# A fused attention and MLP kernel: the order of work at its two changeovers

## The chip, the cores and the metric

One core of a Trainium2 chip. The metric is the device time of one execution in microseconds (us); lower is better. Engines are named as in the profile: PE (TensorE matmul; PEld its weight loads), DVE (VectorE), ACT (ScalarE), POOL (GpSimd) and SP (SyncE, here the queue that issues nearly all DMAs).

## The reference

Random-feature attention, then an MLP with a residual, all float32 in and out (weights arrive as float64 and are decoded in the kernel).

```python
# attention: q, k, v are (8, 8, 576, 64), omega (128, 64)
h = (x * D**-0.25) @ omega.T - sum(x * x) / 2        # for q and for k
phi = exp(h - max(h)) / sqrt(m)
out = phi_q @ (phi_k.T @ v) / (phi_q @ sum(phi_k) + 1e-6)
# mixing and MLP: x is (8, 576, 512), U (576, 32), V (32, 576), w1 (512, 2048), w2 (2048, 512)
u = x + (x.transpose(0, 2, 1) @ U @ V).transpose(0, 2, 1)
return u + maximum(u @ w1, 0) @ w2
```

## The kernel before

**Stages.** Attention runs first, in rounds over pairs of batches and heads. A generator `mixing` (L302) does the U and V products of a pair and stores `u` to memory (`u_dram`, nine chunks of 512 rows). Then comes layer 1 (`u @ w1`, relu), whose result `g` goes to memory (`g_dram`), and layer 2 (`g @ w2` plus `u`).

**Products.** Each float32 product is made of three matmuls of rounded halves: an operand is split into a high part (a cast on ACT, `wh`, `uh`, `gh`) and a low part (value minus high, `wl`, `ul`, `gl`). Both layers use a two-by-two block scheme with 7 products instead of 8 and extra sums: of the left operand S1 to S4 (`SUMS`, L171), of the right operand T1 to T4 (`Right.sums`, L724), and of results. The order of the operands is in `LEFT` and `RIGHT`.

**Layer 1.** Work is cut into units (`unit`, L787) of one chunk c and one weight group g (four groups, NG = 4; nine chunks, NCH = 9). A unit has 7 products of 12 matmuls, 84 in all (L821). DVE adds them (L811), ACT copies and relus (L826, L807), SP stores (L801). Each unit yields after each product, and the caller puts other work there. The order is chunk by chunk, groups 0 to 3. The right operands of a chunk (`prepare`, L749) are 16 loads, 4 transposes on DVE (L768), 4 sums on POOL (L729) and 7 splits (L736, L737); they lie in 8 buffers each of `uh` and `ul`, 7 of them for a chunk.

**Weights.** `decoding` (L101) turns float64 pieces of 128 x 512 into float32: a load (L166) into `raw`, of which there are two buffers (`RB`), two ACT operations (`magnitude`, L114 and L117), three DVE slots (L133, L134, L137) and an addition on POOL (L155). Each call of `advance` does one slot. Four pieces make a group of w1; its operands are 4 sums (L204), 7 casts (L210) and 7 lows (L214) for each of two halves. For groups 0 and 1 sums and lows are on POOL, during attention; for groups 2 and 3 they are on DVE. Group 2's first half is kept in `held` until room for it is free. The 16 pieces of w2 are decoded during layer 1 and go through memory (`w2_dram`).

**First changeover.** `opening` (L848) lays units (0, 0) and (0, 1) between the last mixing steps, with 11 slots of decoding. Unit (0, 2) follows when group 2 is made, (0, 3) when group 3 is.

**Second changeover.** In the last chunk's four units the operands of w2 (`prepare_w2`, L890, and `Right.split`, L733) replace those of w1, one product after another; all four sums are on POOL and the lows alternate between DVE and POOL. When layer 1 is over, the operands of layer 2's first step are made.

**Layer 2.** 36 steps of 7 products and 84 matmuls each (L1043). `Step.split` (L964) makes the operands for the next step while this one runs: a cast on ACT (L976), a low on DVE (L977), S3 and S1 on POOL and S2 and S4 on DVE (L962). S2 is made ahead of split 4 and used in split 5, S4 ahead of split 5 and used in split 6. `Post` (L980) adds the results of two steps to `u` and stores them, between the products of the step after.

**What sets the order.** `K` (`tc.keep_in_program_order`) pins an instruction behind all that was traced before it on its engine. What is not pinned, all DMAs and parts of the decoding among it, may be moved ahead by the framework's scheduler. Each engine then runs its queue strictly in order. PSUM banks come in two sets that alternate from unit to unit (`banks`, L783).

Of the kernel before, what the change touches and what calls it, by code (L numbers as in the profile page):

```python
# [29 lines left out]
def performer_mlp_kernel(ctx: ExitStack, tc, q, k, v, omega, U, V, w1, w2, out):  # L30
# [70 lines left out]
    def decoding(jobs, late, lean):  # L101


        raws, mags, lows = {}, {}, {}

        def fetch(i):
            if i < len(jobs):
                raws[i] = dec.tile([P, PIECE, 2], U32, name="raw", bufs=RB)[:, : jobs[i][1], :]
                jobs[i][0](raws[i])
# [9 lines left out]
        for i in range(RB):  # L119
            fetch(i)  # L120
# [4 lines left out]
        for i, job in enumerate(jobs):  # L125
# [19 lines left out]
            for j, slot in enumerate(slots):  # L145
# [5 lines left out]
                if j == len(slots) - 1:  # L151
                    fetch(i + RB)
# [11 lines left out]
    def weights(src, dest, after):  # L164
        def load(raw):
# [9 lines left out]
    wops, made, held = {}, set(), []  # L175
# [5 lines left out]

    def w1_jobs(g):
        for half in range(2):
            tiles = {}

            def dest(c, tiles=tiles):
                if not tiles:
                    tiles["w"] = dec.tile([P, 2, PIECE], F32, name="wf", bufs=2)
                return tiles["w"][:, c, :]

            def value(name, tiles=tiles):
                w = tiles["w"]
# [6 lines left out]
            engine = nc.gpsimd if g < EARLY_GROUPS else nc.vector

            def total(_, name, value=value, tiles=tiles, engine=engine):
                x, y, op = SUMS[name]
                tiles[name] = dec.tile([P, 2 * P], F32, name="ws", bufs=4)
                engine.tensor_tensor(out=tiles[name], in0=value(x), in1=value(y), op=op)  # L204

            after = [lambda w, name=name, total=total: total(w, name) for name in SUMS]
            for i, name in enumerate(LEFT):

# [9 lines left out]
            if g == EARLY_GROUPS and half == 0:  # L218
                held.extend(after)
                after = []  # L220
# [868 lines left out]
```

## Time and profile before

| | us |
|---|---|
| median of 3 runs | 1136.36 |
| lowest, highest | 1133.68, 1137.52 |
| profiled execution, own time | 1135.71 |
| its span, first to last instruction | 1133.8 |
| mean granted TensorE clock | 0.973 of full |
| busy: PE, DVE, ACT, POOL | 1057.1, 888.8, 612.7, 498.3 |

The span is what the views of the profile cover; the execution's own time has 1.9 us more. A busy share is an average over stages with different limits, so stages are read by their own stretches. "X <- Y" in a list of waits means that X's engine sat idle until Y was done.

### The profile page before, as it was taken

How to read it: one execution, taken by the hardware profiler on the slowest of the kernel's cores; microseconds unless marked ns; L12 is line 12 of the kernel's file. 1: busy time of each engine (PE TensorE's matmuls, PEld its weight loads, DVE VectorE, ACT ScalarE, POOL GpSimd, SP SyncE). 2: the span in 40 equal slices, each digit the busy share in tenths (PEclk: the TensorE clock that was granted, in tenths of full speed). 3: DMA queues.
4: the chain of work that ended last, by engine and by line, in shares of the span. 5: the costliest groups of instructions: out<-in, count | busy, mean ns of one | idle time of the engine just before them, and what ended most of it. 6: DMA issues, size and time to landing. Idle time of an engine off the chain costs nothing. (4 is left out here: it accounts for less than half of the span.)

```text
span 1133.8 us, 23916 instructions
## 1 busy us (share of the span) xinstructions
PE 1057.1 (93%) x8497; PEld 1028.6 (91%) x8497; DVE 888.8 (78%) x1553; ACT 612.7 (54%) x1464; POOL 498.3 (44%) x433
## 2 busy tenths in 40 slices
PE   8989989999988579999999999979999999999998
PEld 7989878899978479899889999869999999999998
DVE  4888899897998885755645555669999999999995
ACT  4878878889863554543433443555443444444441
POOL 3436768737333233123121012575655454554542
PEclk9899999999998789999999999998999999999999
DMA  7788586485245568677666445435453544444351
GB/s 129 142 153 148 95 191 143 89 190 107 81 94 158 161 174 222 168 205 188 188 183 150 119 123 131 143 107 198 144 188 125 172 153 166 170 143 162 143 183 41
DMA packets 374902, 169.25 MB, mean 149 GB/s; under 512 B 275168, under 2 KB 348896, under 8 KB 370176
## 3 DMA queue, kind: packets, MB, share of 16 engines
q1 hardware_dynamic: 374720, 167.67, 55.9%
q8 instruction: 67, 1.10, 0.4%
q14 instruction: 51, 0.42, 0.1%
q0 software_dynamic: 64, 0.07, 0.0%
HBM read 106.86 MB, written 60.82 MB: 148 GB/s over the span
## 5 line engine op out<-in xcount | busy, mean ns | idle before, releaser
L567 ACT ACTIVATE e<-p_p,nm 128x128 f32<-128x128 f32 x576 | 166.5, 386 | 25.0 <-DVE nm L560 15.7
L976 ACT CAST gh<-gs 128x512 fp32r<-128x512 f32 x144 | 89.2, 621 | 151.9 <-DVE gs L962 65.3
L962 POOL TENSOR_TENSOR gs<-graw 128x512 f32<-128x512 f32 x72 | 119.4, 1666 | 112.8 <-DVE gl L977 45.9
L977 DVE TENSOR_TENSOR gl<-gs,gh 128x512 fp32r<-128x512 f32 x144 | 157.1, 1100 | 13.6 <-ACT gh L976 11.7
L433 POOL TENSOR_TENSOR xl<-xT,xh 128x384 fp32r<-128x384 f32 x96 | 100.7, 1065 | 127.5 <-ACT xh L429 99.9
L807 ACT ACTIVATE g<-g 128x512 f32<-128x512 f32 x108 | 68.1, 631 | 152.2 <-DVE g L811 143.9
L560 DVE TENSOR_REDUCE nm<-p_p 128x4 f32<-128x512 f32 x144 | 97.9, 681 | 24.0 <-PE p_p L554 12.0
L155 POOL TENSOR_TENSOR wf<-wf,low 128x512 int32<-128x512 int32 x24 | 34.8, 1450 | 157.4 <-ACT g L807 108.6
L821 PE MATMUL p_n<-uh,wh 128*128 128x256 f32 x304 | 88.5, 291 | 11.5 <-DVE g L811 11.5
L997 POOL TENSOR_TENSOR u<-u,p 128x256 f32<-128x256 f32 x72 | 71.2, 1008 | 62.0 <-DVE u L997 43.1
L552 PE MATMUL p_p<-omh,xh 128*128 128x256 f32 x288 | 93.6, 325 | 1.9 <-ACT e L567 1.6
L976 ACT CAST gh<-graw 128x512 fp32r<-128x512 f32 x108 | 65.4, 620 | 42.8 <-PE p_q L1043 10.7
L821 PE MATMUL p_n<-uh,wl 128*128 128x256 f32 x304 | 87.2, 287 | 0.0
L821 PE MATMUL p_n<-ul,wh 128*128 128x256 f32 x304 | 87.0, 286 | 0.0
L1043 PE MATMUL p_q<-wh,gh 128*128 128x256 f32 x288 | 82.1, 285 | 3.9 <-ACT gh L976 3.9
L977 DVE TENSOR_TENSOR gl<-graw,gh 128x512 fp32r<-128x512 f32 x108 | 81.9, 785 | 4.7 <-ACT gh L976 4.5
L1043 PE MATMUL p_q<-wh,gl 128*128 128x256 f32 x288 | 81.8, 284 | 1.2 <-DVE gl L977 1.2
L554 PE MATMUL p_p<-omh,xl 128*128 128x256 f32 x288 | 82.5, 287 | 0.0
L553 PE MATMUL p_p<-oml,xh 128*128 128x256 f32 x288 | 82.1, 285 | 0.0
L1043 PE MATMUL p_q<-wl,gh 128*128 128x256 f32 x288 | 81.7, 284 | 0.0
L1043 PE MATMUL p_p<-wh,gh 128*128 128x256 f32 x288 | 81.1, 282 | 0.0
L1043 PE MATMUL p_p<-wh,gl 128*128 128x256 f32 x288 | 81.0, 281 | 0.0
(189 smaller groups left out, 3999.0 us busy)
## 6 DMA issues: line engine op xcount, KB each, us to landing
g<-g SPq DMA_DIRECT2D x288, 128.0 KB, 2.4
graw<-g SPq DMA_DIRECT2D x36, 1024.0 KB, 5.2
raw<-in_moe_w_ch_dram SPq DMA_DIRECT2D x32, 512.0 KB, 4.2
u_dram<-ut SPq DMA_DIRECT2D x36, 256.0 KB, 2.3
u<-u_dram SPq DMA_DIRECT2D x36, 256.0 KB, 4.9
out_dram<-u SPq DMA_DIRECT2D x36, 256.0 KB, 2.6
kt<-in_k_dram SPq DMA_DIRECT2D x120, 72.0 KB, 2.7
qt<-in_q_dram SPq DMA_DIRECT2D x120, 72.0 KB, 2.8
```

The costliest lines, as they stand in the source:

```text
L433: nc.gpsimd.tensor_tensor(out=self.xl[-1], in0=self.turned, in1=f32(self.xh[-1]), op=ALU.subtract)
L552: nc.tensor.matmul(o, part.xh[g][:, ts], oh, start=True, stop=False)
L553: nc.tensor.matmul(o, part.xh[g][:, ts], ol, start=False, stop=False)
L554: nc.tensor.matmul(o, part.xl[g][:, ts], oh, start=False, stop=True)
L560: nc.vector.tensor_reduce(out=self.nm[:, :n], in_=self.pp[:, :n], axis=AX.X, op=ALU.max, negate=True)
L567: nc.scalar.activation(out=self.e[:, j, :], in_=self.pp[:, j, :], func=AF.Exp, bias=self.nm[:, j : j + 1])
L821: K(nc.tensor.matmul(p[:, f, :], x[:, k, fs], y[:, k, :], start=first, stop=(k == 1 and y is ul), skip_group_check=True,))
L962: K(engine.tensor_tensor(out=self.val[name], in0=self.val[x], in1=self.val[y], op=op))
L976: K(nc.scalar.copy(out=h, in_=v))
L977: K(nc.vector.tensor_tensor(out=l, in0=v, in1=f32(h), op=ALU.subtract))
L997: K(engine.tensor_tensor(out=out, in0=x, in1=y, op=ALU.add))
L1043: K(nc.tensor.matmul(acc[bank][:, half, :], x[:, ks], y[:, f, :], start=(now.s == 0 and k == 0 and half == 0 and x is h and y is wh), stop ...
```

## The change

- **Order of units.** (0,0), (0,1), (1,0), (1,1), (0,2), (1,2), (0,3), (1,3), then chunk by chunk as before. Chunk 1's operands are made a first time (`guest`), in the buffers meant for group 3's weights, and again for (1,3) in the usual place. Unit (0,1) moves out of the mixing steps.
- **Weights.** Lows of groups 2 and 3 go from DVE to POOL; S3 and S4 overwrite inputs. Group 3's splits wait in `kept` until unit (1,2) releases their buffers, product by product. One slot of decoding per product instead of three; 9 instead of 11 slots in the mixing steps. Each unit asks for operand i just ahead of product i (`w1_need`, `right.need`).
- **Raw pieces.** From the third unit on four raw pieces instead of two: two more lie in the buffer that later holds layer 2's first input.
- **Operands one product apart.** A high part and the low part of the operand before it are issued together; in a chunk's last unit they follow the products that release their buffers. `uh` and `ul` have 7 buffers instead of 8. Sums T1, T3, T2, T4 in this order, T3 in place. Chunk 0's lows alternate between DVE and POOL.
- **Second changeover.** w2's groups are loaded and summed a unit earlier, two of the four sums on DVE; three operands of layer 2's first step are made during units (8,2), its sums during (8,3), the rest during the step itself.
- **Layer 2.** `value` makes a sum when its split asks for it, so S2 comes directly ahead of its cast in split 5, S4 in split 6. The last two steps have the order (0, 4, 1, 2, 3, 6, 5), and the last results are added between the last step's products (`final`).

The diff, cut to its core:

```diff
-        for i in range(RB):
-            fetch(i)
+        fetch(depth())
...
-                    fetch(i + RB)
+                    fetch(i + 1 + depth())
...
+    INPLACE = {"S3": "A21", "S4": "A12"}
+    class Half:
+        def __init__(self, g, half):
+            self.sums, self.lows = (nc.gpsimd, nc.gpsimd) if g < EARLY_GROUPS else (nc.vector, nc.gpsimd)
...
     class Right:
...
+            self.gated = [(0, lambda: self.high(0))]
+            for i in range(1, 7):
+                self.gated += [(i, lambda i=i: self.high(i)), (i, lambda i=i: self.low(i - 1))]
+            self.gated.append((7, lambda: self.low(6)))
...
+        def step(self, gate=7):
+            if self.todo:
+                self.todo.pop(0)()
+            elif self.gated and self.gated[0][0] <= gate:
+                self.gated.pop(0)[1]()
+            else:
+                return False
+            return True
...
     def u_operand(i):
-        return [up.tile([P, 2, HT], F32R, name=n, bufs=8) for n in ("uh", "ul")]
+        return [up.tile([P, 2, HT], F32R, name=n, bufs=UB) for n in ("uh", "ul")]
+
+    UB = 7
...
+    early = prepare(0, ahead, first, lows=(V, G_) * 3 + (V,))
...
     begun = opening()
-    spare = 11
-    for _ in mixers[0]:
-        if spare:
+    spare = 9
...
+    guest = prepare(1, raws, place=w_place(NG - 1), lows=(V, G_) * 3 + (V,), pool=tp)
+    for n, _ in enumerate(mixers[0]):
+        if spare and n % 2:
             advance(decoder, late=True)
             spare -= 1
         next(begun, None)
+        if n > 8 and n % 2:
+            guest.step(-1)
...
+    order = [(0, 0), (0, 1), (1, 0), (1, 1), (0, 2), (1, 2), (0, 3), (1, 3)]
+    order += [(c, g) for c in range(2, NCH) for g in range(NG)]
...
+    def chores(n, i):
+        if n < 2:
+            guest.step()
+            guest.step()
+        if n < 6:
+            for _ in range(3):
+                if held:
+                    held.pop(0)()
+            if not held:
+                advance(decoder, 1, late=True)
+            if n == 5 and {(NG - 1, 0), (NG - 1, 1)} <= ready:
+                for rest in kept.values():
+                    rest.pop(0)()
+                    rest.pop(0)()
+        elif n > 6 and i % 3 == 0:
+            advance(second, 1, late=True)
...
+        for i in unit(c, g, right, banks(n)):
+            chores(n, i)
+            if n == 6:
+                raws = next(ahead2, raws)
+            if c == NCH - 1:
+                if g:
+                    w2_ops[g - 1].step()
+                w2_ops[g].step(i)
+                w2_ops[g].step(i)
+                if g + 1 < NG and i > 2:
+                    w2_ops[g + 1].step(-1)
+                if g == 2 and i % 2:
+                    acts[0].split(len(acts[0].ops))
+                if g == 3 and i < 4:
+                    acts[0].value(("S1", "S2", "S3", "S4")[i])
+            elif nxt:
+                for _ in range(5 if n == 7 else 2 if leaving else 1):
+                    nxt.step(i if leaving else -1)
...
+        def value(self, name):
+            if name not in self.val:
+                for x in SUMS[name][:2]:
+                    self.value(x)
+                self.sum(name, G_ if name in ("S1", "S3") else V)
+            return self.val[name]
...
         def split(self, i):
-            if i == 0:
-                self.sum("S3", nc.gpsimd)
-                self.sum("S1", nc.gpsimd)
-            if i == 4:
-                self.sum("S2", nc.vector)
-            if i == 5:
-                self.sum("S4", nc.vector)
-            o = ORDER[i]
-            h = vp.tile([P, 4 * P], F32R, name="gh", bufs=9)
-            l = vp.tile([P, 4 * P], F32R, name="gl", bufs=9)
-            v = self.val[LEFT[o]]
+            if i == 0 and self.n:
+                self.value("S3")
+                self.value("S1")
+            o = self.order[i]
+            v = self.value(LEFT[o])
+            h, l = self.ops[i] = self.place(i)
             K(nc.scalar.copy(out=h, in_=v))
             K(nc.vector.tensor_tensor(out=l, in0=v, in1=f32(h), op=ALU.subtract))
...
+            if n == 0:
+                if i == 0:
+                    while w2_ops[NG - 1].step():
+                        pass
...
+                    now.split(3)
+                    now.split(4)
+                    acts[1] = Step(1)
+                else:
+                    for _ in range(1 + (i > 2)):
+                        step = now if len(now.ops) < PRODUCTS else acts[1]
+                        if len(step.ops) < PRODUCTS:
+                            step.split(len(step.ops))
```

More of the change, by code (lines that the diff above doesn't have):

```diff
@@ L56, in performer_mlp_kernel @@
     eps = 1e-6 * M
+    K = tc.keep_in_program_order
     def f32(ap):
@@ L199, in w1_jobs @@
[L199 to L207, printed above, removed]
-                def high(_, i=i, name=name, value=value, half=half, g=g):
-                    tc.keep_in_program_order(nc.scalar.copy(out=operand(g, i)[0][:, half, :], in_=value(name)))
-                def low(_, i=i, name=name, value=value, half=half, g=g, engine=engine):
-                    h, l = (x[:, half, :] for x in operand(g, i))
-                    engine.tensor_tensor(out=l, in0=value(name), in1=f32(h), op=ALU.subtract)
-                after += [high, low]
@@ L217, in w1_jobs @@
-            after.append(lambda _, g=g, half=half: made.add((g, half)))
-            if g == EARLY_GROUPS and half == 0:
-                held.extend(after)
-                after = []
+            h = Half(g, half)
+            first, rest = h.after()
+            if g == EARLY_GROUPS and half == 0:
+                held.extend(first + rest)
+                first, rest = [], []
+            if g == NG - 1:
+                kept[half] = rest
+                rest = [lambda h=h: ready.add((h.g, h.half))]
@@ new lines, in sum, with high, low @@
+        def sum(self, name, x, y, engine):
+            to = self.b["B12"] if name == "T3" else self.temps()
+            K(engine.tensor_tensor(out=to, in0=self.b[x], in1=self.b[y], op=ALU.subtract))
+            self.b[name] = to
+        def high(self, i):
+            self.ops[i] = self.place(i)
+            K(nc.scalar.copy(out=self.ops[i][0], in_=self.b[RIGHT[i]]))
+        def low(self, i):
+            h, l = self.ops[i]
+            K(self.lows[i].tensor_tensor(out=l, in0=self.b[RIGHT[i]], in1=f32(h), op=ALU.subtract))
+            self.ready.add(i)
@@ L740, in performer_mlp_kernel, with need @@
+        def step(self, gate=7):
[6 more added lines that the diff above has]
+            return True
+        def need(self, i):
+            while i not in self.ready:
+                self.step()
+    V, G_ = nc.vector, nc.gpsimd
     phase = ctx.enter_context(ExitStack())
     up = phase.enter_context(tc.tile_pool(name="up", reuse_waits="tile", bufs=1))
+    late = {}
@@ L760, in load, with loads @@
+    def loads(c, pool):
+        raws = []
+        for cc in range(NC):
+            raws.append(pool.tile([P, PAIR], F32, name="uraw", bufs=NC))
             for a in range(4):
@@ L999, in steps @@
             q = {f"{h + 1}{j + 1}": self.u[h][:, j * HT : (j + 1) * HT] for h in range(2) for j in range(2)}
-            m1 = vp.tile([P, HT], F32, name="p1", bufs=1)
+            if last:
+                yield from self.final(add, q)
+                return
+            m1 = late["vp"].tile([P, HT], F32, name="p1", bufs=1)
             K(nc.scalar.copy(out=m1, in_=self.m("A11")))
@@ L1036, in performer_mlp_kernel @@
             bank, half = BANK[i]
-            o = ORDER[i]
+            o = now.order[i]
             for k in range(4):
@@ L1052, in performer_mlp_kernel @@
             next(post, None)
-        if now.s == 1:
+        if n == 0:
+            while len(acts[1].ops) < PRODUCTS:
+                acts[1].split(len(acts[1].ops))
+        if now.s == 1 and not last:
             for _ in post:
```

361 lines of the change are left out of this document (211 added, 150 removed).

## The prediction

> **What bounds the kernel now.** I read the page first, then the busy time by stretch, the waits, and last the instructions in order of time at three places.
>
> The page says TensorE: 93% busy, and its slices dip in two places.
>
> ```profile
> PE 1057.1 (93%) x8497; PEld 1028.6 (91%) x8497; DVE 888.8 (78%) x1553; ACT 612.7 (54%) x1464; POOL 498.3 (44%) x433
> PE   8989989999988579999999999979999999999998
> ```
>
> The busy time by stretch (columns: length, then busy of PE, PEld, DVE, ACT and POOL with counts, then granted clock, DMA share, GB/s). I cut it where runs of 84 matmuls begin: 84 make one unit of layer 1 or one step of layer 2.
>
> ```profile
> 342.46:358.75 16.29, 15.03 (x91) 13.98 (x90) 14.69 (x24) 6.97 (x13) 5.58 (x4) 0.73 0.51 170
> 358.75:417.02 58.27, 37.62 (x254) 35.94 (x253) 46.49 (x86) 28.47 (x62) 17.11 (x12) 0.85 0.60 164
> 417.02:460.76 43.74, 40.59 (x338) 40.01 (x337) 26.55 (x46) 21.31 (x37) 10.27 (x8) 1.00 0.72 189
> 460.76:712.22 251.46, 244.35 (x2018) 242.31 (x2017) 138.52 (x216) 103.99 (x180) 49.96 (x38) 0.99 0.63 163
> 712.22:765.74 53.52, 42.84 (x338) 41.43 (x337) 34.50 (x41) 28.44 (x54) 35.91 (x26) 0.96 0.46 133
> 765.74:779.21 13.47, 12.22 (x85) 11.93 (x85) 13.47 (x16) 6.32 (x12) 7.34 (x5) 0.80 0.71 252
> 779.21:1128.93 349.72, 349.71 (x2942) 349.51 (x2940) 321.95 (x433) 150.65 (x258) 181.02 (x139) 1.00 0.43 150
> 1128.93:1133.80 4.87, 0.00 (x0) 0.00 (x0) 1.50 (x4) 0.00 (x0) 1.23 (x2) 0.92 0.29 108
> ```
>
> Layer 2 after its first step is 35 steps in 349.72 us, TensorE busy throughout: 9.99 us for 84 matmuls is the floor. Against it:
> - units 0 to 7 (342.46 to 460.76): 118.3 us for 79.9, 38.4 lost, most of it in units 1 to 3 (58.27 for 30.0)
> - units 8 to 31: 251.5 for 239.8, 11.7 lost
> - units 32 to 35 with the gap and layer 2's first step: 67.0 for 50.0, 17.0 lost
> - the tail: 4.87
>
> The waits name the causes (engine and line, what it waited for: us in total, times, longest); the first four rows are from 342 to 418, the last from 418 to 640.
>
> ```profile
> PE p_n L821 <- DVE g L811: 8.7, 2, 8.0
> PE p_p L821 <- ACT wh L210: 5.4, 2, 3.7
> ACT wf L114 <- DMA raw<-in_moe_w_ch_dram: 18.5, 6, 5.5
> ACT low L117 <- DMA raw<-in_moe_w_ch_dram: 3.0, 2, 2.2
> ACT low L117 <- DMA raw<-in_moe_w_ch_dram: 23.7, 10, 4.0
> ```
>
> Units 2 and 3 need weight groups that are still being decoded, and ScalarE, in order, stands before raw pieces that have not landed. In later units the same wait travels on; here at the end of chunk 1 (start, length, engine, what, idle before):
>
> ```profile
> 451.51 0.66 ACT L117 ACTIVATE low<-raw 128x512 int32<-128x512 uint32 x1 [4.05 <-DMA raw<-in_moe_w_ch_dram]
> 455.03 0.69 DVE L737 TENSOR_TENSOR ul<-ts,uh 128x512 fp32r<-128x512 f32 x1 [6.83 <-ACT uh L736]
> ```
>
> 4.05 us on the DMA, then VectorE idle 6.83 us for a cast behind it in ScalarE's queue.
>
> **The prices.** Means from the groups by line and shape, 342 to 760 (count, busy us, mean ns, then idle), and the 256-wide weight lows on both engines (ns min/median/max).
>
> ```profile
> L811 DVE TENSOR_TENSOR g<-p_n,u 128x512 f32<-128x512 f32 x57 | 38.7, 684 | 16.6 <-PE p_n L821 14.7 <-DMA g<-g 0.7
> L737 DVE TENSOR_TENSOR ul<-ts,uh 128x512 fp32r<-128x512 f32 x36 | 29.9, 832 | 32.8 <-ACT uh L736 32.8
> L768 DVE STREAM_TRANSPOSE uT<-uraw 128x512 f32<-128x512 f32 x32 | 22.4, 700 | 2.0 <-DMA uraw<-u_dram 2.0
> L737 DVE TENSOR_TENSOR wl<-wf,wh 128x512 fp32r<-128x512 f32 x6 | 7.1, 1184 | 11.6 <-ACT wh L736 11.6
> L137 DVE SCALAR_TENSOR_TENSOR wf<-raw,wf 128x512 uint32<-128x512 uint32 x23 | 15.7, 682 | 0.1
> L133 DVE TENSOR_SCALAR wf<-wf 128x512 f32<-128x512 f32 x22 | 12.6, 571 | 1.9 <-ACT wf L114 1.9
> L134 DVE TENSOR_SCALAR wf<-wf 128x512 uint32<-128x512 uint32 x23 | 12.0, 523 | 0.1
> L204 DVE TENSOR_TENSOR ws<-wf 128x256 f32<-128x256 f32 x8 | 3.3, 412 | 0.0
> L155 POOL TENSOR_TENSOR wf<-wf,low 128x512 int32<-128x512 int32 x24 | 34.8, 1450 | 157.4 <-ACT g L807 108.6 <-DVE wf L137 45.4 <-DMA uraw<-u_dram 3.3
> L729 POOL TENSOR_TENSOR ts<-uT,ts 128x512 f32<-128x512 f32 x16 | 21.1, 1320 | 2.4 <-DVE uT L768 1.8
> L737 POOL TENSOR_TENSOR wl<-ts,wh 128x512 fp32r<-128x512 f32 x10 | 12.9, 1292 | 11.4 <-ACT wh L736 11.4
> L214 POOL TENSOR_TENSOR wl<-ws,wh x16: 717/734/1191, 120.8 to 337.9; 128x256 fp32r<-128x256 f32 x16
> L214 DVE TENSOR_TENSOR wl<-ws,wh x16: 413/416/426, 372.0 to 402.9; 128x256 fp32r<-128x256 f32 x16
> ```
>
> A unit costs VectorE 5 adds, 3.4 us; a piece of decoding 0.57 + 0.52 + 0.68 = 1.8 us there and 1.45 on GpSimd.
>
> **Part 1, units 0 to 7.** Chunk 1's units of groups 0 and 1 now run before any unit needs groups 2 and 3, so group 2 has two more units (20 us) to be made in, group 3 three or four. The price: chunk 1's operands are made twice. The extra set is 4 transposes and 4 lows on VectorE (2.8 + 3.3 us), 4 sums and 3 lows on GpSimd (5.3 + 3.9), 7 casts on ScalarE (28.47 of 58.27 us busy there) and 16 more loads on SP's queue, which nothing orders and which can go out early. The 28 weight lows go from VectorE (28 x 0.416 = 11.6 us) to GpSimd (28 x 0.734 = 20.6).
>
> Counted in program order, VectorE is given in units 1 to 3: 15 adds (10.3), 4 chunk-1 lows (3.3), 11 weight sums (4.5), 5 pieces (8.9), 27.0 us for 30 us of matmuls. GpSimd gets 2 sums, 3 lows, 14 weight lows and 6 additions: 2.6 + 3.9 + 10.3 + 8.7 = 25.5. Each fits alone. But they get in each other's way (rows under part 4: a low of 0.68 takes 1.72 us beside a GpSimd sum): some 28 VectorE operations on SBUF, GpSimd busy 85% of the time, half an operation (0.45) each, are 10.7 us, VectorE then 7.7 over. Matmuls may run three products (4.3 us) ahead of the adds, so 3.4 to 7.7 are lost; I take 5.5. Unit 0 keeps its 6.3 (it starts while the mixing ends). Units 4 to 6: 1.5. Unit 7 is given chunk 2's whole preparation: adds 3.4, transposes 2.8, 7 lows 5.8, one piece 1.8 = 13.8, 3.8 over, half of it covered by the same lead: 2. Loss 15.3 instead of 38.4: **-23.1**. Ends: -32.1 (unit 0's loss alone stays) and -8 (only the one wait of 8.0 goes).
>
> **Part 2, units 8 to 31.** Four raw pieces instead of two give a piece some 30 us to land. The ScalarE wait goes; late next is VectorE at each chunk's last unit: 3.4 + 7 x 0.83 + 1.8 = 11.0 for 9.99, four times. 3.7 stays of 11.7: **-8**. Ends: 0 and -11.7.
>
> **Part 3, layer 2's opening.** Two of the four weight sums per group move from GpSimd (busy 35.91 of 53.52 us in that stretch) to VectorE, sums are issued a unit earlier, and three operands of layer 2's first step are made two units ahead. VectorE by unit: 32: adds 3.4, 4 lows 4.8, 4 sums at about 1.0, one left-over low 0.8 = 13; 33: 10.2; 34: 10.2 + 3 lows of the first step at 1.1 = 13.5; 35: 3.4 + 4.8 + 2 sums 1.8 = 10. The step itself needs four more lows, 5.6, inside its 9.99. Sum 56.7; with 2.3 for waits between the engines 59 instead of 67: **-8**. Ends: +3 (VectorE's extra sums end last, nothing saved) and -17.
>
> **Part 4, every step of layer 2.** The change moves the sums S2 and S4 (VectorE, L962) each from one product ahead of its use to directly before it. VectorE, ScalarE and GpSimd around there:
>
> ```profile
> 889.00:908.99 19.99, 19.99 (x171) 19.99 (x170) 18.79 (x26) 8.77 (x15) 9.68 (x8) 1.00 0.45 151
> 899.40 0.68 DVE L977 TENSOR_TENSOR gl<-gs,gh 128x512 fp32r<-128x512 f32 x1
> 903.32 0.68 DVE L962 TENSOR_TENSOR gs<-gs,graw 128x512 f32<-128x512 f32 x1
> 904.12 1.72 DVE L977 TENSOR_TENSOR gl<-gs,gh 128x512 fp32r<-128x512 f32 x1
> 905.77 0.68 DVE L962 TENSOR_TENSOR gs<-graw,gs 128x512 f32<-128x512 f32 x1
> 904.00 1.29 POOL L962 TENSOR_TENSOR gs<-graw 128x512 f32<-128x512 f32 x1 [6.01 <-DVE gs L962]
> 906.55 0.63 ACT L976 CAST gh<-gs 128x512 fp32r<-128x512 f32 x1 [1.07 <-DVE gs L962]
> 907.73 1.41 PE p_m L1043 x12
> ```
>
> Now the low of S1 runs on VectorE while ScalarE casts S2. After the change the queue is S2, its cast, its low, S4, its cast, its low, so VectorE, in strict order, stands 0.10 + 0.63 + 0.04, about 0.8 us, behind each sum (0.85 with the lost overlap of two operations). It has 19.99 - 18.79 = 1.2 us to spare in two steps. Fully exposed, two steps take 18.79 + 4 x 0.85 = 22.2. But GpSimd's next S1 is released when S2 is done; its 1.29 us would then lie in the first of these idle stretches rather than on a low. So I take one exposed wait a step: 18.79 + 1.7 = 20.5, 0.5 over in two steps, 17 times 8.8 us. The lead absorbs part: the last low of the step begun at 899.09 ends at 900.08, its product starts at 907.73, 7.6 us. The opening will have used about 3 of them: 8.8 - 4.6 = **+4**. Ends: 0 (more of GpSimd's work falls into the gaps) and 17 x 2.2 - 4.6 = +33.
>
> **Part 5, the tail.** In before the last add follows GpSimd:
>
> ```profile
> 1128.05 2.10 POOL L997 TENSOR_TENSOR u<-u,p 128x256 f32<-128x256 f32 x3 [4.46 <-DVE p L997]
> 1130.19 0.42 DVE u L997
> ```
>
> With S2 earlier and the adds between the products one add (0.42) follows the last matmul at 1128.93: -1.1. Against it, three times a product writes one half of a bank whose other half is just being read; no row shows such a pair, bounds 0 and three adds with their handshakes, +2.5. Taken **+0.5**.
>
> **Sum.** -23.1 - 8 - 8 + 4 + 0.5 = -34.6. The profiled execution took 1135.71 us (span 1133.8), 0.65 below the median of the three runs: 1135.7 - 34.6 = 1101.
>
> **Rivals.**
> 1. *More is hidden:* part 1 at -30, part 3 at -11, part 4 at 0: 1135.7 - 30 - 8 - 11 + 0.5 = 1087. For it: VectorE and GpSimd each fit. Against: 46.49 of 58.27 us busy there already.
> 2. *The first changeover becomes GpSimd's.* The lows cost the two engines 20.6 - 11.6 = 9.0 us more and the extra chunk-1 work 9.2 on GpSimd; if none falls beside idle time that is 18.2 instead of my 5.5: 1101 + 12.7 = 1114. For it: ScalarE then also waits for weight buffers that GpSimd has not emptied.
> The Trainium skill (SBUF — State Buffer, section "SBUF: two separate sides") says that the port shared by the two engines is an exclusive lock, held for a whole instruction. By that rule, moving lows to GpSimd is moving them to the slower holder of the same lock, as in this rival; the trace agrees, since the low of 904.12 ended 0.55 us after the sum of 904.00 did.
> 3. *Layer 2 becomes VectorE's* (the slower side). Both waits of part 4 exposed: +33 instead of +4, 1130. The gaps can also lower TensorE's clock: the first step above ran 12.22 us busy at a clock of 0.80, 2.2 over. If every second pair of steps draws that, two steps cost 3.3 over: 17 x 3.3 - 4.6 = 51.5, 1149. It ends slower than before by more than 0.3% from 2.75 us over per pair.
> 4. *The deeper raw queue does nothing,* because pieces are late for lack of bandwidth (0.63 DMA share): part 2 at 0, 1109.
>
> **How the numbers follow.** 0.3% of 1136, or 3.4 us, is about what a measurement of this kernel can tell from no change. Chances: forecast (1091 to 1111) 0.55, rival 1 (1074 to 1091) 0.15, rival 2 0.12, rival 3 0.14, rival 4 0.04. Of rival 3, 0.05 is faster, 0.03 within 0.3%, 0.06 slower; all others are faster: 0.91, 0.03, 0.06. The range leaves out the lower half of rival 1 and the upper part of rival 3: 1080 to 1128.
>
> **What would show it.** Right: units 1 to 3 near 12 us, no ScalarE wait over 2 us on raw pieces after unit 3, layer 2's first step under 11 us. Part 4: layer 2's 84-matmul steps stay at 9.99 at first and stretch later, with VectorE idle before the lows of S2 and S4. Wrong: steps over 10.5 us from the start, or units 1 to 3 over 15.

## The result and the profile after

The changed kernel takes 1117.61 us (median of 4 runs, 1115.4 to 1119.08), the kernel before 1136.37 on the same chip: ratio 0.9837, 95% interval 0.9812 to 0.9861. It is faster by 18.8 us; 34.6 were forecast. Its profiled execution took 1116.97 us, 18.7 less than that of before.

The page of the changed kernel, busy time by engine and TensorE's slices:

```profile
PE 1053.7 (94%) x8497; PEld 1025.6 (92%) x8497; DVE 858.7 (77%) x1538; ACT 597.3 (54%) x1471; POOL 529.9 (48%) x463
PE   8989988999988798999999999989999999999996
```

The first dip (slices 14 and 15) is shallower, the second (slice 27) nearly gone, and the last slice is emptier. VectorE is busy 30 us less, GpSimd 32 us more.

The changed kernel by stretch (columns as in the prediction), cut at unit 0, units 1 to 3, 4 to 7, 8 to 31, 32 to 35, layer 2's first step, steps 1 to 34, the last step and the tail:

```profile
341.62:355.38 13.76, 13.18 (x89) 11.79 (x88) 12.44 (x18) 4.90 (x10) 8.06 (x8) 0.89 0.46 152
355.38:399.50 44.12, 35.82 (x255) 35.21 (x254) 36.44 (x52) 22.52 (x47) 28.99 (x27) 0.85 0.61 160
399.50:445.29 45.79, 41.20 (x339) 40.31 (x337) 30.83 (x48) 24.27 (x50) 23.72 (x23) 0.98 0.79 188
445.29:693.82 248.53, 243.40 (x2017) 242.17 (x2017) 150.64 (x234) 107.27 (x191) 55.47 (x42) 0.99 0.69 180
693.82:740.80 46.98, 41.61 (x338) 40.91 (x337) 38.51 (x50) 26.98 (x51) 28.09 (x20) 0.96 0.45 129
740.80:750.67 9.87, 9.87 (x86) 9.80 (x84) 4.58 (x7) 5.07 (x11) 2.47 (x3) 1.00 0.79 260
750.67:1093.19 342.52, 341.42 (x2858) 340.13 (x2857) 290.55 (x423) 135.92 (x256) 187.28 (x136) 1.00 0.46 156
1093.19:1111.55 18.36, 12.06 (x86) 11.26 (x84) 8.48 (x18) 3.07 (x6) 5.79 (x7) 0.91 0.08 29
1111.55:1115.20 3.65, 0.00 (x0) 0.00 (x0) 0.42 (x1) 0.00 (x0) 0.00 (x0) 1.00 0.38 144
```

Against before, in the prediction's parts:

| part | before | after | difference | forecast |
|---|---|---|---|---|
| start to unit 0 | 342.5 | 341.6 | -0.8 | 0 |
| 1: units 0 to 7 | 118.3 | 103.7 | -14.6 | -23.1 |
| 2: units 8 to 31 | 251.5 | 248.5 | -2.9 | -8 |
| 3: units 32 to 35 and first step | 67.0 | 56.9 | -10.1 | -8 |
| 4: steps 1 to 34 | 339.7 | 342.5 | +2.8 | +4 |
| 5: last step and tail | 15.0 | 22.0 | +7.1 | +0.5 |

Parts 3 and 4 came close to the forecast. What is missing lies in parts 1, 2 and 5: 8.5, 5.1 and 6.6 us. In these places the trace of the changed kernel shows the following.

**The last step** takes 18.36 us for 10.06 us of matmuls. In order of time (start, length, engine, what, idle before it):

```profile
1097.05 0.87 DVE L1014 TENSOR_TENSOR gs<-graw,gs 128x512 f32<-128x512 f32 x1
1098.03 0.62 ACT L1040 CAST gh<-gs 128x512 fp32r<-128x512 f32 x1 [2.99 <-DVE gs L1014]
1098.56 0.61 ACT L1040 CAST gh<-graw 128x512 fp32r<-128x512 f32 x1
1098.68 0.69 DVE L1041 TENSOR_TENSOR gl<-gs,gh 128x512 fp32r<-128x512 f32 x1 [0.76 <-ACT gh L1040]
1099.08 0.36 ACT L1141 COPY p<-p_q 128x256 f32<-128x256 f32 x1
1099.49 0.58 PE L1183 MATMUL p_q<-wh,gh 128*128 128x256 f32 x1 [4.72 <-ACT p L1141]
1104.40 0.39 PE L1183 MATMUL p_q<-wh,gh 128*128 128x256 f32 x1 [0.52 <-DVE p L1109]
```

The step's first product ends at 1094.77. The second writes the other half of the same bank p_q, so it waits for ScalarE's copy of the first half. That copy stands behind two casts of the step's own operands, and the first of them waited 2.99 us for a sum on VectorE, which is late. TensorE stands 4.72 us, then twice more for a reader of the other half (0.52, and 1.06 ahead of a product in p_kv), and it is busy 12.06 us for 10.06: its matmuls behind the first gap are slow for some 3 us (0.41 us apiece in place of 0.28), and around each gap matmuls that otherwise overlap stand alone. Together 4.72 + 0.52 + 1.06 + 2.0 = 8.3.

**Units 8 to 31** lose most in units 16, 20 and 24, the first of a chunk (12.5, 13.6, 11.8 us). The list of waits from 446 to 694:

```profile
ACT wf L132 <- DMA w_dram<-wf: 67.8, 13, 7.9
```

The waits on raw pieces are gone, as forecast. In their place ScalarE waits for a buffer wf, until the store of an earlier decoded piece has read it. At unit 16:

```profile
524.34 0.51 SPq L183 DMA_DIRECT2D graw<-in_moe_w_ch_dram  x1
524.95 0.46 SPq L258 DMA_DIRECT2D w_dram<-wf  x1
530.86 0.67 ACT L132 ACTIVATE wf<-raw 128x512 f32<-128x512 f32 x1 [4.15 <-DMA w_dram<-wf]
532.66 0.69 DVE L772 TENSOR_TENSOR ul<-ts,uh 128x512 fp32r<-128x512 f32 x1 [3.35 <-ACT uh L768]
```

The store is issued behind two raw loads of 512 KB and lands 5.9 us later; the casts uh stand behind the Abs in ScalarE's queue, VectorE idles 3.35 us for them, and TensorE 2.05 us for the copy of its first product, which ScalarE makes after them.

**Units 1 to 3** took 44.1 us where 35.5 were forecast (30.0 and 5.5 lost). Units 1 and 2 by themselves:

```profile
355.38:373.02 17.64, 13.01 (x87) 12.80 (x86) 13.80 (x18) 10.32 (x23) 12.72 (x12) 0.81 0.55 160
373.02:388.83 15.81, 12.51 (x86) 12.31 (x85) 13.04 (x17) 5.31 (x13) 12.65 (x13) 0.79 0.56 155
```

TensorE's gaps: 4.63 us in unit 1 ahead of product 4, 3.30 in unit 2 ahead of product 5, small ones in unit 3, which takes 10.7. ScalarE around the first:

```profile
364.19 0.66 ACT L132 ACTIVATE wf<-raw 128x512 f32<-128x512 f32 x1 [4.22 <-DMA raw<-in_moe_w_ch_dram]
365.32 0.57 ACT L878 COPY g<-p_q 128x512 f32<-128x512 f32 x1
```

Product 4 adds to the bank that this copy must read first, and the copy stands behind the Abs (L132) of a late piece. That piece's load was issued at 359.66, 2.2 us after VectorE had last read the piece two before (until 357.51), and landed 4.5 us later. The second gap ends at an add on VectorE, which is behind: it is busy without a pause from 373.4 to 385.0 and waits for GpSimd before and after that. Four rows of the list of waits, 341 to 446:

```profile
ACT wf L132 <- DMA raw<-in_moe_w_ch_dram: 7.6, 2, 4.2
ACT low L135 <- DMA raw<-in_moe_w_ch_dram: 6.1, 2, 4.6
DVE wf L221 <- POOL wl L229: 3.7, 3, 2.0
PE p_n L873 <- DVE g L861: 3.5, 2, 3.3
```

The granted clock, cut where it changes, and once more at 358.40:

```profile
344.75:358.40 13.65, 13.21 (x106) 12.56 (x105) 12.56 (x20) 5.38 (x11) 6.41 (x6) 1.00 0.43 135
358.40:365.23 6.83, 2.90 (x25) 2.70 (x23) 6.01 (x7) 2.05 (x4) 5.75 (x5) 1.00 0.90 267
365.23:372.06 6.83, 6.12 (x28) 6.13 (x29) 4.68 (x7) 6.83 (x17) 5.29 (x7) 0.50 0.27 82
372.06:382.30 10.24, 8.19 (x70) 7.98 (x68) 8.93 (x12) 3.98 (x8) 8.19 (x8) 1.00 0.45 128
382.30:389.12 6.82, 5.57 (x26) 5.58 (x27) 4.20 (x7) 2.58 (x7) 5.70 (x6) 0.50 0.74 194
```

Behind each gap the clock is at a half for 6.8 us. TensorE is busy 13.0 us in unit 1 and 12.5 in unit 2 for some 10 us of work, so gap and clock together seem to make 7.6 and 5.8 us; experiment 7 tests whether the clock's part counts. Its changes (344.75, 365.23, 372.06, 382.30, 389.12) lie 6, 2, 3 and 2 times 3.41 us apart. The Trainium skill (TensorE: Matmul & The Clock Gate, section "Part 1: The HAM clock gate") states that the clock is judged in free-running windows of about 3.4 us and halved after an idle one. The spacing agrees, and so does the first gap, which fills the whole 3.41 us ahead of 365.23. The second does not: in the 3.41 us ahead of 382.30 TensorE was still busy for 1.36 us, and the half clock followed all the same.

### The profile page after: what moved, and what is told of

Same layout as the page of the kernel before. It is cut to its first block, busy times and chain, and to the rows that moved or that the text cites. A ratio compares the mean times of both kernels' runs of the same rounds, so it can differ in the third digit from the quotient of the medians.

```text
span 1115.2 us, 23932 instructions
## 1 busy us (share of the span) xinstructions
PE 1053.7 (94%) x8497; PEld 1025.6 (92%) x8497; DVE 858.7 (77%) x1538; ACT 597.3 (54%) x1471; POOL 529.9 (48%) x463
## 5 line engine op out<-in xcount | busy, mean ns | idle before, releaser
L1040 ACT CAST gh<-gs 128x512 fp32r<-128x512 f32 x140 | 83.2, 619 | 209.8 <-DVE gs L1014 179.1
L1014 POOL TENSOR_TENSOR gs<-graw 128x512 f32<-128x512 f32 x70 | 113.9, 1648 | 111.4 <-DMA graw<-g 81.4
L1041 DVE TENSOR_TENSOR gl<-gs,gh 128x512 fp32r<-128x512 f32 x140 | 114.3, 827 | 53.5 <-ACT gh L1040 53.5
L1109 POOL TENSOR_TENSOR u<-u,p 128x256 f32<-128x256 f32 x72 | 80.5, 1145 | 59.6 <-DVE u L1109 56.1
L538 PE MATMUL p_n<-kv,eT 128*128 128x65 f32 x512 | 74.0, 271 | 8.0 <-ACT eT L523 5.8
L538 PEld LDWEIGHTS p_n<-kv,eT 128*128 128x128 f32 x512 | 67.9, 193 | 12.4 <-ACT eT L523 6.5
L873 PE MATMUL p_n<-uh,wh 128*128 128x256 f32 x272 | 77.4, 284 | 1.6 <-DVE g L861 1.6
L873 PE MATMUL p_n<-uh,wl 128*128 128x256 f32 x272 | 77.0, 283 | 1.4 <-POOL wl L229 1.4
L1041 DVE TENSOR_TENSOR gl<-graw,gh 128x512 fp32r<-128x512 f32 x107 | 75.2, 731 | 4.0 <-ACT gh L1040 4.0
L1183 PE MATMUL p_p<-wh,gh 128*128 128x256 f32 x276 | 77.8, 282 | 0.0
```

Source lines behind the costliest of these rows:

```text
L538: nc.tensor.matmul(pn[:, h, :], eT[:, h, :], kv[:, h, s // 5, :], start=True, stop=True)
L873: K(nc.tensor.matmul(p[:, f, :], x[:, k, fs], y[:, k, :], start=first, stop=(k == 1 and y is ul), skip_group_check=True,))
L1014: K(engine.tensor_tensor(out=to, in0=self.val[x], in1=self.val[y], op=op))
L1040: K(nc.scalar.copy(out=h, in_=v))
L1041: K(nc.vector.tensor_tensor(out=l, in0=v, in1=f32(h), op=ALU.subtract))
L1183: K(nc.tensor.matmul(acc[bank][:, half, :], x[:, ks], y[:, f, :], start=(now.s == 0 and k == 0 and half == 0 and x is h and y is wh), stop ...
```

## The experiments

Each was compared with the kernel before on its own chip. Where the code of a stretch is the same, profiles still differ: units 0 to 7 took 102.9 to 105.1 us in the five kernels whose edits lie behind them (the changed kernel and those of experiments 1, 2, 3 and 5). So medians of a few us apart say little, and each verdict rests on the stretch that its edit touches, in one profile of each kernel.

**1. The old order of the last two steps** (the changed kernel with one part undone).

```diff
-    ORDERS = [(0, 4, 5, 2, 3, 1, 6)] * (NCH * 2 - 1) + [(0, 4, 1, 2, 3, 6, 5)]
+    ORDERS = [(0, 4, 5, 2, 3, 1, 6)] * (NCH * 2)
...
-        last = n == NS - 1
+        last = False
```

> The changed kernel, but the last two steps of layer 2 keep the old order of products and the last results are added after the last product, as before the change. In the changed kernel the last step takes 18.35 us instead of 9.99 (PE waits 4.72 us for ScalarE's copy of its first product, the other half of whose bank the second product writes). Theory (readers between products of one bank, with ScalarE and VectorE late): last step 10 to 11 us, then 4.9 us of tail, 6 to 7.5 us less than the changed kernel, about 1111. Rival (the last step's own operands are late because VectorE lags, the adds only stand behind that): last step still 14 us or more, at most 3 us less, 1115.

Measured: 1111.41 us, ratio 0.9793 (0.9738 to 0.9847). Its last step and tail:

```profile
1095.82:1105.88 10.06, 10.06 (x86) 9.86 (x84) 7.40 (x16) 1.51 (x3) 4.52 (x6) 1.00 0.15 55
1105.88:1110.78 4.90, 0.00 (x1) 0.00 (x0) 1.51 (x4) 0.00 (x0) 1.23 (x2) 0.90 0.29 107
```

8.3 us less in the step, 1.25 more in the tail: the new end costs 7.1 us. This is shown for its two parts together, the order of the products and the additions between them; they were not tried apart.

**2. Each split makes the next split's S2 or S4 ahead of its own cast** (part 4 undone within the new code).

```diff
             v = self.value(LEFT[o])
+            if self.n and i < 6 and LEFT[self.order[i + 1]] in ("S2", "S4"):
+                self.value(LEFT[self.order[i + 1]])
             h, l = self.ops[i] = self.place(i)
```

> The changed kernel, but each split of layer 2 makes the S2 or S4 that the next split needs ahead of its own cast, as before the change; the new tail stays. Theory (VectorE idles 0.8 us behind each of the two sums and so lags by most of its lead): steps 1 to 34 fall from 342.5 to about 340 us, the low of a step's last operand is made within 2.5 us of the step's start instead of 5, ScalarE's copy in the last step comes earlier and its gap falls from 4.72 to under 1.5: 6 to 8 us less, about 1110. Rival (the lag comes from the opening and never heals, whatever the sums' place): steps and gap stay, within 1.5 us of 1117.6.

Measured: 1112.55 us, ratio 0.9803 (0.9752 to 0.9853). Two steps of the changed kernel, then steps 1 to 34 and the last step of this one:

```profile
889.99:909.97 19.98, 19.98 (x171) 19.98 (x170) 16.92 (x26) 7.84 (x16) 11.01 (x8) 1.00 0.45 155
```

```profile
749.97:1089.89 339.92, 339.92 (x2858) 339.77 (x2857) 324.25 (x433) 149.66 (x259) 187.24 (x137) 1.00 0.44 156
1089.89:1102.85 12.96, 10.86 (x86) 10.04 (x84) 2.55 (x6) 0.37 (x1) 2.89 (x4) 1.00 0.05 17
```

Steps 1 to 34 have no gap left. What that saves is less sure than 342.5 against 339.9 says: with part 4 in place the same steps took 340.7 to 342.8 us in seven profiles. The last step keeps its order and falls from 18.4 to 13.0: with VectorE no longer late, the gap of 4.72 becomes 0.52:

```profile
1091.99 0.38 PE L1185 MATMUL p_q<-wh,gh 128*128 128x256 f32 x1 [0.52 <-ACT p L1143]
```

What stays are three waits for readers of the same bank, 2.1 us together, and 0.8 us more busy time around them; the granted clock is 1.00 here, but matmuls of 0.28 us that otherwise start 0.12 us apart stand alone at each gap. So VectorE's lag from part 4 is what made the new order of the end dear.

**3. Four places for decoded pieces of w2**: a piece of w2 fills half of a buffer wf, so two pieces share one.

```diff
+    def w2_tile(f):
+        if f // 2 not in pairs:
+            pairs[f // 2] = dec.tile([P, 2, PIECE], F32, name="wf", bufs=2)
+        return pairs[f // 2][:, f % 2, :]
...
-        return weights(w2[f * P : (f + 1) * P, :], piece_tile, [store])
+        return weights(w2[f * P : (f + 1) * P, :], lambda: w2_tile(f), [store])
```

> The changed kernel, but the decoded pieces of w2 lie in the two halves of each wf buffer, four places instead of two. In the changed kernel ScalarE no longer waits for raw pieces in units 8 to 31, but 67.8 us in 13 waits for the store of the piece decoded two earlier. Theory (the wait moved from the raw load to that store): the 67.8 us go, units 8 to 31 fall from 248.5 to 241 to 244 us, 5 to 7 us less, about 1112. Rival (the losses at chunks' first units are VectorE's load or the new operands' order): units 8 to 31 stay within 1.5 us, 1117.

Measured: 1116.92 us, ratio 0.9807 (0.977 to 0.9845). Units 8 to 31, and ScalarE's wait from 445 to 712:

```profile
449.65:693.25 243.60, 241.10 (x2018) 240.15 (x2017) 147.94 (x234) 110.14 (x190) 55.42 (x42) 1.00 0.70 184
ACT wf L132 <- DMA w_dram<-wf: 11.9, 3, 5.1
```

The stretch is 4.9 us shorter, the wait 67.8 to 11.9 (12.4 us more at the same line are put down to other transfers). Six profiles with the old code of this stretch gave 248.1 to 252.4, so 243.6 is clear of them. The time did not follow: the theory's 1112 failed, the median hardly moved, and in the profiled execution the start, units 0 to 7 and the opening, which the edit doesn't touch, came out 2.9, 1.4 and 2.0 us longer. The mechanism is shown; its worth in the whole time rests on experiment 5.

**4. Two raw pieces throughout** (the deeper raw queue undone).

```diff
     def depth():
-        return 2 * RB if roomy else RB
+        return RB
...
-        if roomy and n >= 0 and n // 2 % 2:
+        if False:
```

> The changed kernel with two raw pieces throughout instead of four from the third unit on. Theory (four pieces only moved the wait from the load to the store): ScalarE waits for raw pieces again, 15 us or more in units 8 to 31, fewer waits on stores, units 8 to 31 within 2.5 us of 248.5; units 0 to 7 within 2 us; total within 3 us of 1117.6. Rival (the deeper queue is what units 8 to 31 gained by): they go to 252 or more, units 0 to 7 also longer as groups 2 and 3 are late, 1123 or more.

Measured: 1130.91 us (10 runs), ratio 0.9947 (0.992 to 0.9973). Units 8 to 31, and waits from 445 to 712:

```profile
454.68:712.37 257.69, 245.03 (x2018) 242.18 (x2018) 149.45 (x233) 109.12 (x191) 56.33 (x42) 0.99 0.67 173
ACT low L135 <- DMA raw<-in_moe_w_ch_dram: 67.6, 14, 9.3
ACT wf L132 <- DMA w_dram<-wf: 11.9, 12, 2.1
```

The theory that the deeper queue had only moved the wait from piece to store fell; the rival was right, by the median too, which is 13.3 us above the changed kernel's. With one slot of decoding per product and two pieces the stretch takes 257.7 us, 6 more than before: in the new order the four pieces are worth 9.2 us here, or 5.3 against the longest of the profiles with four. This profile is the slowest of the ten executions (1137.48), but 6.3 us of its excess lie in the start, which the edit doesn't touch. The two rows also show that the total of a wait is a poor price: ScalarE waits some 68 us in one kernel for pieces, in the other for stores, and TensorE loses 17.9 of units 8 to 31 in the one and 8.7 in the other.

**5. The three edits of 1, 2 and 3 together.**

> Three edits of the earlier runs together: the last step keeps the order of the other steps, each split makes the next split's S2 or S4 ahead of its own cast, and the decoded pieces of layer 2's weights have four places. Theory (the three costs lie in different stages and add up): units 8 to 31 take 243 to 245 us, steps 1 to 34 339 to 341 us, the last step 10 to 10.5 us and the tail 4.9 us, so the stages save 4.9 + 2.6 + 8.2 - 1.2 = 14.5 us against the changed kernel: 1101 to 1105 us. Rival (what units 8 to 31 gain is given back in layer 2's opening, which waits for the last decoded pieces anyway: the run with four places alone came out only 0.7 us shorter): the opening grows from 56.9 to 60 to 62 us, and the run takes 1107 to 1110 us.

Measured: 1105.77 us (1104.54 to 1108.65), ratio 0.9725 (0.9688 to 0.9762).

```profile
448.22:690.16 241.94, 240.68 (x2019) 239.99 (x2018) 148.39 (x235) 110.44 (x191) 55.32 (x42) 1.00 0.71 186
748.93:1089.04 340.11, 340.11 (x2858) 339.79 (x2857) 323.12 (x434) 149.87 (x259) 188.73 (x137) 1.00 0.44 156
1089.04:1099.10 10.06, 10.06 (x86) 9.85 (x84) 1.37 (x4) 0.37 (x1) 1.61 (x3) 1.00 0.07 26
```

The stretches save what the theory said and a little more (6.6 + 2.4 + 8.3 - 1.25 = 16.1 us); start, units 0 to 7 and the opening came out 4.8 us longer in this profile, as in others with the same code there. The time lies between the theory's range and the rival's; the opening took 58.8, not the rival's 60 to 62. The interval lies wholly below that of the changed kernel. This version beats both.

What is left against the floor is the first changeover, units 0 to 7: 104.6 us for 79.9. The other runs look for its cause.

**6. Three edits of the changed kernel in units 1 to 3.** Lows of groups 2 and 3 back on VectorE; another place for ScalarE's wait on the raw piece; S4 on the engine that makes A12's low:

```diff
-            self.sums, self.lows = (nc.gpsimd, nc.gpsimd) if g < EARLY_GROUPS else (nc.vector, nc.gpsimd)
+            self.sums, self.lows = (nc.gpsimd, nc.gpsimd) if g < EARLY_GROUPS else (nc.vector, nc.vector)
```

> The low parts of weight groups 2 and 3 are made on VectorE, where the changed kernel makes them on GpSimd; nothing else differs. Theory (units 1 and 2 are held by the order in which VectorE reaches its work, and VectorE has no room: it is busy 13.8 of 17.6 us in unit 1 and 13.0 of 15.8 us in unit 2): some eight lows of 128x256 for each group, at 0.4 to 0.7 us each, come on top of it, and units 0 to 7 take 106 to 112 us (103.7 in the changed kernel); the run is 2 to 8 us slower than the changed kernel. Rival (the first changeover is GpSimd's, whose lows take 0.77 to 0.87 us each and stand in the way of VectorE's work beside them): the three stalls on GpSimd's lows go, units 1 and 2 fall to 13 to 15 us each, units 0 to 7 to 97 to 101 us, and the run is 3 to 7 us faster than the changed kernel.

```diff
-    spare = 9
+    spare = 7
```

> The point from which the decoder may start one slot earlier is 7 where the changed kernel has 9, so that ScalarE meets the Abs of a late raw piece at another place of unit 1. Theory (unit 1's 17.6 us come from ScalarE's 4.2 us in front of an Abs whose raw piece is on its way, and its copy g stands behind it): the wait moves away from the copy, the 4.6 us gap of TensorE shrinks to under 2 us, unit 1 takes 14 to 15.5 us and units 0 to 7 100 to 102 us. Rival (the piece is late wherever it is asked for, and VectorE's and GpSimd's queues in unit 1 set its end): unit 1 stays between 17 and 18.5 us, and units 0 to 7 between 103 and 105 us.

```diff
-            self.sums.tensor_tensor(out=to, in0=self.v[x], in1=self.v[y], op=op)
+            (self.lows if name == "S4" else self.sums).tensor_tensor(out=to, in0=self.v[x], in1=self.v[y], op=op)
```

> S4 of weight groups 2 and 3, which is written in place of A12, is made on GpSimd, which also makes A12's low; in the changed kernel VectorE makes it and waits for that low (2.0 us once, 3.7 us in three places). Theory (that wait of VectorE holds the unit behind it): VectorE is free 3 to 5 us earlier over units 1 and 2, unit 2 falls from 15.8 to 13 to 14.5 us, and units 0 to 7 to 100 to 103 us. Rival (GpSimd is busy 12.6 of 15.8 us in unit 2 and 12.7 of 17.6 us in unit 1, and four additions of 0.8 to 1.5 us more make it the last): the operands come later, unit 2 takes 16 to 18 us, and units 0 to 7 104 to 107 us.

Measured: 1129.89, 1119.33 and 1120.69 us; ratios 0.9935 (0.9912 to 0.9959), 0.9837 (0.9795 to 0.9879) and 0.9857 (0.9812 to 0.9902). Units 0 to 7 took 112.4, 103.2 and 104.0 us. The first settles the prediction's second rival: with the lows off GpSimd the stretch grows by 8.7 us (units 1 to 3 take 47.4, unit 6 17.2), so their move to GpSimd pays; the whole run lost 12.3 us, more than the theory's 2 to 8. In the second unit 1 falls to 15.7, which neither had, and unit 3 rises from 10.7 to 12.2; the sum is the rival's. In the third unit 2 takes 16.1, as the rival said, and nothing is gained. Both theories on single waits fell: what is taken away in unit 1 or 2 comes back in the next.

**7. TensorE kept busy over both gaps**, on top of experiment 5: 32 matmuls into the next unit's bank ahead of product 4 of unit 1 and product 5 of unit 2.

```diff
+    FILL = {1: 4, 2: 5}
...
+            p = banks(n + 1)[0]
+            for q in range(32):
+                K(nc.tensor.matmul(p[:, 0, :], x[:, 0, :P], y[:, 0, :], start=q == 0, stop=False, ...))
```

> On top of the three edits together (1105.8 us; units 0 to 7 104.6 us, unit 1 16.9 us with a gap of 4.4 us ahead of its product 4, unit 2 15.5 us with a gap of 3.7 us ahead of its product 5), TensorE gets 32 more matmuls ahead of each of those two products, into the bank that the next unit opens afresh, so that they change no result; at full clock they take 3.8 us each time, about the length of the gap. Theory (each of the two gaps costs more than itself, because the granted clock goes to a half for 3.4 to 6.8 us right behind it, 2.4 us more in unit 1 and 1.7 us more in unit 2): the clock stays at 0.95 or above over both units, unit 1 takes 14 to 15 us, unit 2 13 to 14.5 us, units 0 to 7 100 to 102 us. Rival (operands are late, not products: with a full clock TensorE only waits longer for VectorE and GpSimd, whose work in these units is as long as before): the clock is at 0.95 or above too, but units 0 to 7 take 103.5 to 106 us, and new gaps stand behind the added matmuls.

Measured: 1106.45 us, ratio 0.9715 (0.9674 to 0.9757). Unit 1 (from 0.1 us behind its start), unit 2, then units 1 to 3 together:

```profile
359.97:374.87 14.90, 14.22 (x118) 13.99 (x117) 13.25 (x18) 7.60 (x17) 10.13 (x9) 1.00 0.54 160
374.87:391.17 16.30, 14.74 (x118) 13.92 (x117) 12.02 (x17) 8.62 (x20) 13.14 (x14) 1.00 0.64 181
359.87:405.04 45.17, 40.66 (x319) 39.42 (x317) 37.42 (x53) 22.85 (x47) 29.72 (x28) 0.96 0.65 169
```

The clock now stays at 1.00 through both units, so the gaps did lower it. Unit 1 gains 1.9 us (15.0) and still waits 0.68 behind the added matmuls. But units 2 and 3 take 16.3 and 13.9, unit 3 with a new gap of 2.26 and 3.4 us at half clock, and units 0 to 7 105.6 us: the rival was right, the clock's part is given back to the other engines' work, which comes no sooner. In unit 2 no gap follows the added matmuls, so their own 3.9 us might have been the delay. The trace speaks against it: they end at 388.15, and the addition on VectorE for which product 5 had waited 3.7 us in experiment 5 ends at 388.09 here (`g <- p_n, u`, 387.41 for 0.68).

**8. The late groups' work spread over units 2 to 6**, on top of experiment 5.

```diff
         if n < 6:
+            if n < 2:
+                return
             for _ in range(3):
```

> On top of the three edits together, the hand-written order gives unit 1 (and the part of unit 0 behind the last layer of before) no work on the late weight groups: sums, casts, lows and decoding of groups 2 and 3 are issued from unit 2 on, between products as before, and whatever is missing is issued where a unit asks for it. Theory (units 1 and 2 hold 13 to 14 us of VectorE's work each where units 4 to 6 hold 5.6 to 8 us, so that the same work spread later fits beside the products): unit 1 falls from 16.9 to 11 to 13.5 us, units 2 to 5 grow by 1 to 3 us together, and units 0 to 7 take 100 to 102.5 us. Rival (the chain of decode, sums, casts and lows of group 2, which unit 4 needs, is as long as the three units it has now): the stall moves to unit 4 or 5, which takes 15 to 20 us, and units 0 to 7 take 104 to 109 us.

Measured: 1109.53 us, ratio 0.9754 (0.9716 to 0.9792). Units 1 to 3, then 4 to 7:

```profile
354.41:390.49 36.08, 31.62 (x254) 31.42 (x253) 27.16 (x39) 17.52 (x37) 22.68 (x23) 0.95 0.70 186
390.49:449.92 59.43, 45.24 (x338) 43.61 (x337) 40.66 (x61) 30.67 (x63) 27.99 (x29) 0.86 0.66 153
```

Units 2 and 3 now run at 9.9, but unit 6, the first that needs group 3, takes 22.6: 109.7 us together. The rival was right in kind, with the stall in unit 6 instead of 4 or 5. Unit 1 still takes 16.3 us, but it was not emptied: sums and an Abs of pieces begun during the mixing still run there, VectorE is busy for 13.8 us as in the changed kernel, and ScalarE waits 4.1 us for a raw piece in front of that Abs. The theory on VectorE's work in unit 1 is therefore not tested by this run.

**9. One engine's work left out**, on top of experiment 5: VectorE's clamp, or GpSimd's addition, for the eight late pieces of w1.

```diff
+                if base < 0:
+                    slots[0] = None
...
```

> On top of the three edits together (1105.8 us, units 0 to 7 104.6 us), the decoder leaves out VectorE's clamp of the magnitudes for the eight late pieces of layer 1's weights; in the changed kernel these eight took 8.0 us of VectorE between 341 and 400 us (8 at 999 ns, 0.42 us where GpSimd is idle and up to 1.5 us beside it). Theory (VectorE's queue sets when the operands of units 1 to 7 are there): units 0 to 7 lose 5 to 8 us and take 97 to 100 us. Rival (GpSimd's queue sets it, VectorE waits for its lows and additions): units 0 to 7 stay between 102.5 and 105 us.

```diff
-            nc.gpsimd.tensor_tensor(out=whole(m), in0=whole(m), in1=e, op=ALU.add)
+            if i < lean or base >= 0:
+                nc.gpsimd.tensor_tensor(out=whole(m), in0=whole(m), in1=e, op=ALU.add)
```

> On top of the three edits together, GpSimd's addition of the small part to the decoded magnitude is left out for the same eight pieces; in the changed kernel these eight took 10.3 us of GpSimd between 341 and 400 us (8 at 1289 ns). The weights lose their last bits by it. Theory (GpSimd's queue sets when the operands are there, by its own work and by what it stretches on VectorE beside it): units 0 to 7 lose 6 to 11 us and take 94 to 99 us. Rival (VectorE's queue sets it, and GpSimd's additions lie beside it): units 0 to 7 lose less than 2.5 us and take 102 to 105 us.

Measured: 1103.03 and 1107.91 us, ratios 0.9709 (0.9662 to 0.9756) and 0.9756 (0.9709 to 0.9803); units 0 to 7 102.7 and 104.0 us. Taking away 8.0 us of VectorE's operations gains 1.9 there, 10.3 us of GpSimd's 0.6, no more than five kernels with the same code differ by (2.3). Both rivals' ranges held and both theories fell: neither kind of operation by itself sets the end of the first changeover. For VectorE the test is weaker than it looks: its busy time in units 0 to 7 fell by 3.6 us only (78.5 to 74.9), since operations that came next took longer (the shift, L151, 654 ns in place of 484). GpSimd's fell by the full 10.2.

This stays open. What the kernels of experiments 6 (the second), 7, 8 and 9 share with the changed one is a wait of ScalarE for a raw piece in unit 1 or 2, of 3.6 to 5.5 us at the longest. Until the third unit there are two raw pieces, so each is loaded once the one two before it has been read. That this chain of load, decode and load sets the pace is the candidate left, argued from that wait and not shown; a deeper queue in these units was not tried. Two more things were not tried by themselves: the new order of the units and the new opening of layer 2, so what parts 1 and 3 gained is read from the stretches as a whole.

## Why the prediction was right or wrong

The direction and the range (1080 to 1128) held. The point was 16.6 us too low, and 1117.6 lies outside the 1091 to 1111 to which the forecast itself gave 0.55. Two of the signs by which it was to be judged went against it: units 1 and 2 took 17.6 and 15.8 us, where "units 1 to 3 over 15" was to show it wrong, and in unit 4 ScalarE still waited 4.6 us for a raw piece. Layer 2's signs held in the main: its first step took 9.87 us, and VectorE idles ahead of the lows of S2 and S4.

- **Part 1** (-23.1, measured -14.6). VectorE's busy time came out as counted: 27.0 + 10.7 = 37.7 us for units 1 to 3, and it was busy 36.4. Part of that is luck, since 52 operations ran there, not the 45 counted (three transposes of chunk 1 and an addition of the mixing, 2.7 us, among the rest). GpSimd was counted at 25.5 and had 29.0. The step that failed is the next one, "VectorE then 7.7 over", less a lead of three products. It takes VectorE as working without a pause. It idled 7.7 us of the 44.1, waiting for ScalarE, GpSimd and matmuls in turn, and the lead could not be used: product 4 of a unit waits for ScalarE's copy of its product 0, and ScalarE stood before a raw piece, the very wait that the prediction quoted from before and let go. Units 1 to 3 lost 14.2, not 5.5. Unit 0 lost 3.8, not 6.3; unit 7 3.7, not 2.
- **Part 2** (-8, measured -2.9). That four pieces end the raw wait was right, and in experiment 4 the stretch without them is longer than before. The failed sentence is "late next is VectorE at each chunk's last unit". Late next was a store whose buffer ScalarE needed, at the first units of three chunks (units 16, 20 and 24); with four buffers the term is -7.9 (experiment 3) or -9.5 (experiment 5).
- **Part 3** (-8, measured -10.1, 56.9 us). The forecast of 59 is the upper part of what nearly the same code gave in all kernels, 56.9 to 59.3.
- **Part 4** (+4, measured +2.8). Both waits of a step are exposed, not one, at 0.76 us each, but VectorE's work in two steps fell from 18.79 to 16.92 us: 16.92 + 4 x 0.76 = 19.96 against 19.98 of matmuls, where 20.5 was forecast. So the steps hardly stretch, but a lag once taken is not worked off. Of the 2.8 us, 1.5 come in step 1, which waits for its input to land; other profiles of the same code gave +0.9 to +3.1.
- **Part 5** (+0.5, measured +7.1). The tail fell by 1.2 as counted, and the waits between halves of a bank (0.52 + 1.06) lie inside the bound of 2.5. What failed is that parts 4 and 5 were priced apart: part 4's lag was called covered by a lead of 7.6 us, and part 5 let a copy in the last step depend on ScalarE, whose casts depend on that lagging VectorE. Experiments 1 and 2 each remove one of the two, and most of the cost goes with either: 7.1 and 5.4 us in these stretches.

Of the rivals, the second (GpSimd's changeover, 1114) was nearest in time and wrong in mechanism: experiments 6 and 9. The third (layer 2 becomes VectorE's) did not come: 342.5 us for 34 steps. The fourth was refuted by experiment 4.

## What to carry to other kernels

A lead that covers a small lag covers it only as long as nothing in the last stage depends on the late engine: price a reordering of the end together with the lag that arrives there. When a queue is made deeper, look up which buffer its consumer needs next and when the transfer that frees it is issued. And in this case a slower clock behind a gap cost little, because the other engines were not ready for faster matmuls: that can be tested by filling the gap, if the trace then shows what the next product waited for.

## What the hardware showed that was not expected

- An exposed wait of VectorE cost almost nothing, because its other operations became shorter. In layer 2 the same lows took 1107 ns apiece before, 830 in the changed kernel and 1104 in experiment 2, which puts S2 and S4 back ahead; S4's sum gives a part back (1147 ns before, 1631 in the changed kernel). That it is GpSimd's sums falling into VectorE's waits is read from the trace, not tested: two of them run for 3.48 us from 894.78, while VectorE idles 0.77 us ahead of 896.13. The groups by line and shape of before (779 to 1118), of the changed kernel (751 to 1093) and of experiment 2 (750 to 1090):

```profile
L977 DVE TENSOR_TENSOR gl<-gs,gh 128x512 fp32r<-128x512 f32 x139 | 152.7, 1107 | 13.6 <-ACT gh L976 11.7
```

```profile
L1041 DVE TENSOR_TENSOR gl<-gs,gh 128x512 fp32r<-128x512 f32 x136 | 111.3, 830 | 51.9 <-ACT gh L1040 51.9
```

```profile
L1043 DVE TENSOR_TENSOR gl<-gs,gh 128x512 fp32r<-128x512 f32 x140 | 153.3, 1104 | 10.8 <-ACT gh L1042 9.1
```

- A store of 256 KB issued 0.6 us behind a load of 512 KB on SP's queue took 5.9 us to land. The 16 stores of this kind took 2.8 to 7.8 us, 4.4 at the median, where the output's stores of the same size take 2.2. That the loads ahead of them are the reason is not shown.
